# A first layer norm on rows of x, moved by selection matrices, and a first inverse stage in 64-column tiles

## The chip, the core and the metric

The kernel runs on one core of a Trainium2 chip. The metric is device time in microseconds (us). TensorE (PE) does matmuls, VectorE (DVE), ScalarE (ACT) and GpSimd (POOL) do elementwise work, SyncE (SP) issues most DMAs.

## The reference, cut to what matters

One block of a network with 2048 tokens of 512 channels: an adaptive layer norm, a long convolution per channel (an S4 layer, its kernel K made from 128 complex exponentials per channel), a second adaptive layer norm, and a feed-forward part with squared ReLU.

```python
mod = (silu(c) @ w_mod).reshape(1, 6, 1, 512)
sa, ca, ga, sb, cb, gb = mod[:, 0], ..., mod[:, 5]
h = layernorm(x) * (1 + ca) + sa               # over the 512 channels
# S4, per channel d:
P = exp(dt * A * l)                            # l = 0 .. 2047, 128 states
K = real(sum_n C * P * dt * B)
y = irfft(rfft(pad(h)) * rfft(pad(K)))[:2048] + h * Dskip
x = x + ga * y
h = layernorm(x) * (1 + cb) + sb
x = x + gb * (relu(h @ w1 + b1) ** 2 @ w2 + b2)
```

## The kernel before, in words

**Layout.** The 2048 tokens are written as 32 x 64 (a and b), and the convolution is done by two-stage transforms written as matmuls. In the layout of the transforms, a partition holds one a of one of four groups of channels, and along the free dimension stand 128 channels times 64 values of b. In the layout of rows, a partition holds one token and the free dimension its 512 channels; there are sixteen such row tiles of 128 tokens (`rows`, loaded from `xt`). The buffer `big1` holds x in the transforms' layout (`xj`, and `x_sb[c]` for one of eight blocks of 16 channels). `big0` first holds the parameters of the convolution kernel; later both hold results of the inverse transform.

**Statistics and modulation.** Mean and variance come from the row tiles (L507 to L514: bn_stats on DVE, square root on ACT). Sixteen small matmuls with slices of an identity move them to the transforms' layout (L518, L523). x itself is loaded a second time, in the transforms' layout, from `x4` (`load_x`, four loads of 1 MB). The modulation vectors come from `mod_rows` (L540), 16 matmuls with 32-column tiles each; three are needed early, three later (`late_modulation`, which also loads the last one's weights).

**Scaling.** `scale(c)` applies the layer norm to one block of 1024 elements a partition: three DVE instructions (L603 to L605) and one on POOL (L606). The gain ga / 2048 is folded in.

**Convolution kernel.** It is made in 32 units, four to a group. For each unit POOL adds the phases (L712) and multiplies three amplitude arrays (L734); ACT takes two sines (L721 to L723); DVE multiplies (L740 to L744); PE contracts over the 128 states (L751) into one half of the bank `kg`; ACT copies to `ksb` (L824), and the first transform stage follows (`stage1`, L615, evacuated at L617). Per group POOL builds integer phase tables (L684) and ACT takes 24 exponentials (L703). Buffers: three for amplitudes, two for phases, two `ksb`, three PSUM banks `ps` used in turn by everything from modulation to inverse stage, and seven `xy` buffers for rows, modulation weights and spectra, handed out by `spectrum()` and given back to the list `spectra`.

**Transforms and inverse.** `u_pieces(c)` scales a block of x and transforms it (L615, L625). `product_pieces(c)` does the second stage of the kernel's spectrum (L625), multiplies the spectra on DVE (L761) and does the first inverse stage (L769: in each bank eight matmuls with 128 columns, copied out by two ACT copies, L773). Four banks make a block, eight blocks in all. The second inverse stage (L937), the second layer norm and the feed-forward part (L1031 to L1061) follow; they make up the time from about 360 us to the end.

**The order of the work.** `background()` places the pieces of x and of the products among the 32 units, by hand-written positions. This fixes the order in which buffers are handed out. Then `keep_order` replans every engine's order: a list scheduler with a cost for each instruction (`weight`), which takes of the ready groups the one with the longest way to the end, plus a bonus (`hurry`, in ns) for some. SP's queue takes, of what is ready, the first in the order of the program. The plan is added as fixed dependencies, so each engine works through its list in order and a waiting instruction holds up all behind it.

Of the kernel before, what the change touches and what calls it, by code (L numbers as in the profile page):

```python
# [17 lines left out]
L = 2048  # L18
# [77 lines left out]
def weight(ins):  # L96
# [3 lines left out]
    if "DMA" in type(ins).__name__:  # L100
# [12 lines left out]
            tiles = 128 // cols if cols in (32, 64, 128) else 1  # L113
            t = 2.2 * max(moving / 1.2 / tiles + 2, {128: 112, 64: 28}.get(cols, 13))
            return t, t + 170
# [10 lines left out]
            if n <= 4:  # L126
                t = 200
        case "Pool":
            t = 110 + 1.8 * n
        case _:  # L130
# [4 lines left out]
def keep_order(tc, traced, slots, in_turn, whole, urgent):  # L135
# [85 lines left out]
    for g, n in enumerate(left):  # L221
        if n == 0:
            ready[of[g][0]].append(g)
    landed = table = 0
    WINDOW = 3413
# [9 lines left out]
    for _ in groups:  # L235
# [6 lines left out]
        cost = takes[g][0]  # L242
        if e == "PE":
            cost /= level(now)
            a = now
            while a < now + cost - 1:
                w = int(a // WINDOW)
                b = min(now + cost, (w + 1) * WINDOW)
                busy[w] = busy.get(w, 0) + b - a
                a = b  # L250
        elif e == "DVE" and shares_port(groups[g][0]):
            cost += min(650, max(0, free["Pool"] - now))
        elif e == "Activation":
# [23 lines left out]
def tile_adaln_ssm_ffn(  # L277
    ctx: ExitStack,
    tc: tile.TileContext,
    x4: bass.AP,  # L280
    xt: bass.AP,
# [62 lines left out]
    ctile("apart", [P, 24])  # L344

# [165 lines left out]
    mean = ctile("mean", [P, 64])  # L511
    rstd = ctile("rstd", [P, 64])
    nc.scalar.activation(mv1[:, :, 1], mv1[:, :, 1], AF.Sqrt, bias=epsb)
    nc.vector.reciprocal(mv1[:, :, 1], mv1[:, :, 1])  # L514
    mp = bank("ps", PS)
# [5 lines left out]
    moved = mp[:, 0:128].rearrange("p (g s t) -> p s g t", g=4, t=2)  # L521
    for i, t in enumerate((mean, rstd)):
        nc.vector.tensor_copy(t.rearrange("p (s g) -> p s g", g=4), moved[:, :, :, i])  # L523
    hurry(mark, 60000)

    for _ in parameters(1, NC - 1):
        pass

# [8 lines left out]
    def mod_rows(wm, ps):  # L537
        for q in range(4):
            for kc in range(4):
                nc.tensor.matmul(  # L540
                    ps[32 * q : 32 * q + 32, 0:128], srep[:, 32 * kc : 32 * kc + 32], wm[:, kc, 128 * q : 128 * q + 128],
                    start=(kc == 0), stop=(kc == 3))
# [5 lines left out]

    srep, gs = (cst.tile([P, 128], F32, tag=n, name=n) for n in ("srep", "gs"))
    nc.vector.tensor_copy(srep.rearrange("p (k x) -> p k x", k=4), bc(sl, 2, 32))  # L550
# [28 lines left out]
    nc.sync.dma_start(b1c, b1.rearrange("(t p) -> p t", p=P))  # L579
    load_x(2)  # L580
    wm_sb, wm_cb = (wm_next() for _ in range(2))
    load_x(4)
    load_x(6)

    def late_modulation():
# [12 lines left out]
        spectra.extend(wms[3:])  # L598


    def scale(c):
        ds = slice(16 * c, 16 * c + 16)
        nc.vector.tensor_sub(x_sb[c], x_sb[c], bc(mean, 1, 16))  # L603
        nc.vector.tensor_mul(x_sb[c], x_sb[c], bc(rstd, 1, 16))
        nc.vector.tensor_mul(x_sb[c], x_sb[c], bc(g4[:, ds], 2, 64))  # L605
        nc.gpsimd.tensor_add(x_sb[c], x_sb[c], bc(s4[:, ds], 2, 64))  # L606


# [146 lines left out]
    def product_pieces(c):  # L755
# [9 lines left out]
        for g in range(4):  # L765
            ps = bank("ps", PS)
            for i in range(4):
                for h, y in ((0, yu), (1, yr)):
                    nc.tensor.matmul(  # L769
                        ps[:, 128 * i : 128 * i + 128], pairs(y)[:, g, i // 2, :, i % 2],  # L770
                        e1_sb[:, h], start=(h == 0), stop=(h == 1))
            for r in range(2):
                nc.scalar.copy(  # L773
                    z4[r][c][:, :, 4 * g : 4 * g + 4].rearrange("p j d -> p d j"),
                    ps.rearrange("p (d r j) -> p d r j", d=4, r=2)[:, :, r])
# [307 lines left out]
def laid_out(inputs):  # L1083
# [41 lines left out]
```

## Time and profile before

| | |
|---|---|
| Median of 3 runs | 712.5 us (709.61 to 714.19) |
| Profiled execution | 709.58 us, its span 707.8 us, mean granted PE clock 0.928 |
| PE busy | 596.5 us (84%) |
| PE weight loads busy | 516.4 us (73%) |
| DVE busy | 392.0 us (55%) |
| ACT busy | 380.0 us (54%) |
| POOL busy | 345.3 us (49%) |
| Chain that ended last | PE 63%, POOL 20%, DMA 5%, DVE 5%, ACT 5% |

A busy share is an average over stages with different limits, so the stretches of the span are read one by one. A group of instructions is listed by line, engine, operation, output and inputs with their shapes, count, then busy us and mean ns of one, then the idle time of the engine before them and what ended it. "L12" is line 12 of the kernel. The chain of waits goes back from the last instruction, at each step to what released it. The granted PE clock is a share of the full one.

### The profile page before, as it was taken

The page shows a single profiled execution, that of the slowest core. Times are in us where ns is not written, and L with a number is a line of the kernel's source. Part 1 is how long each engine was busy: PE and PEld are TensorE (multiplying, and loading weights), DVE is VectorE, ACT ScalarE, POOL GpSimd, SP SyncE. Part 2 cuts the span into 40 slices and gives each one's busy share as a digit, 9 for nine tenths or more (in the row PEclk, how much of TensorE's full clock was granted, in tenths as well). Part 3 has the DMA queues.
Part 4 walks back from the last instruction along what each step waited for, and adds up shares of the span by engine and source line. Part 5 has one row for each costly group of instructions (what it writes and reads, how often), then busy time and mean ns, then how long its engine had stood idle before and what let it go on. Part 6 is the DMA issues. An engine that isn't in the chain of part 4 may idle for free.

```text
span 707.8 us, 18955 instructions
## 1 busy us (share of the span) xinstructions
PE 596.5 (84%) x8306; PEld 516.4 (73%) x8306; DVE 392.0 (55%) x622; ACT 380.0 (54%) x760; POOL 345.3 (49%) x316
## 2 busy tenths in 40 slices
PE   1321695766989999999868999999999999999996
PEld 1311584765989889999846788888888888888884
DVE  5788889975677576861245784243332533252233
ACT  3464867555999999875626464223432334222220
POOL 5768999999798798740969571000100000000000
PEclk9855798888999999999977999999999999999998
DMA  9990002020202022353822220001000100010001
GB/s 328 374 362 10 3 2 63 1 61 2 63 4 63 18 48 62 106 132 82 288 89 63 77 74 1 1 0 60 0 1 1 60 1 1 0 46 15 1 1 59
DMA packets 22274, 46.38 MB, mean 66 GB/s; under 512 B 3760, under 2 KB 9264, under 8 KB 20400
## 3 DMA queue, kind: packets, MB, share of 16 engines
q1 hardware_dynamic: 21760, 45.04, 20.4%
q8 instruction: 65, 1.06, 0.6%
q10 hardware_dynamic: 432, 0.14, 0.1%
q14 instruction: 17, 0.14, 0.1%
HBM read 32.58 MB, written 4.19 MB: 52 GB/s over the span
## 4 chain that ended last, share of the span: by engine, by line
PE 63%; POOL 20%; DMA 5%; DVE 5%; ACT 5%; issue 3%; DVEq 0%; SPq 0%; POOLq 0%; ACTq 0%
PE tg L1051 7%; PE tg L1053 7%; PE tg L1052 7%; PE ps L769 6%; PE ps L1031 6%; PE ps L1032 6%; PE ps L1034 5%; POOL rtl L734 5%; POOL tables L684 5%; PE ps L625 5%; POOL llph L712 4%; PE ps L615 3%; PE tg L937 2%; PE kg L751 2%; DMA xy<-xt 2%
## 5 line engine op out<-in xcount | busy, mean ns | idle before, releaser
L1039 DVE TENSOR_TENSOR xy<-xy 128x512 f32<-128x512 f32 x56 | 43.9, 784 | 158.9 <-ACT rw L1038 107.6
L1037 ACT ACTIVATE xy<-ps,b1c 128x512 f32<-128x512 f32 x42 | 29.0, 690 | 130.7 <-PE ps L1034 130.7
L966 POOL TENSOR_TENSOR big<-big,b2g 128x512 f32<-128x512 f32 x16 | 21.1, 1318 | 157.7 <-DVE xy L964 153.4
L734 POOL TENSOR_TENSOR rtl<-tables 128x512 f32<-128x512 f32 x75 | 83.9, 1142 | 8.7 <-issue 5.7
L625 PE MATMUL ps<-xy,t_sb 128*64 128x64 f32 x2048 | 71.0, 228 | 10.8 <-DVE xy L761 6.6
L769 PE MATMUL ps<-e_sb,xy 128*128 128x128 f32 x512 | 70.9, 296 | 8.4 <-ACT big L773 5.5
L625 PEld LDWEIGHTS ps<-xy,t_sb 128*64 128x64 f32 x2048 | 67.0, 143 | 14.1 <-DVE xy L761 6.9
L769 PEld LDWEIGHTS ps<-e_sb,xy 128*128 128x128 f32 x512 | 65.5, 204 | 12.0 <-ACT big L773 5.9
L712 POOL TENSOR_TENSOR llph<-tables 128x1024 int32<-128x1024 int32 x32 | 65.1, 2034 | 15.5 <-ACT tg L723 15.3
L617 ACT COPY xy<-ps 128x512 f32<-128x512 f32 x64 | 36.7, 590 | 18.9 <-PE ps L615 18.4
L743 DVE TENSOR_TENSOR rtl<-rtl,tg 128x1024 f32<-128x1024 f32 x32 | 38.9, 1217 | 14.2 <-ACT tg L723 13.4
L721 ACT ACTIVATE tg<-llph 128x1024 f32<-128x1024 int32 x32 | 33.1, 1034 | 25.0 <-POOL llph L712 20.4
L761 DVE TENSOR_TENSOR xy<-ps,xy 128x512 f32<-128x512 f32 x64 | 39.7, 681 | 7.1 <-DMA xy<-xy 6.3
L615 PE MATMUL ps<-d_sb,ksb 128*64 128x128 f32 x512 | 34.2, 281 | 7.1 <-ACT xy L617 4.2
L773 ACT COPY big<-ps 128x256 f32<-128x256 f32 x64 | 33.9, 626 | 10.4 <-PE ps L769 10.4
L615 PE MATMUL ps<-d_sb,big 128*64 128x128 f32 x512 | 33.7, 280 | 5.2 <-DVE xy L761 4.5
L723 ACT ACTIVATE tg<-llph,halfpi 128x1024 f32<-128x1024 f32 x32 | 36.0, 1126 | 1.5 <-DVE llph L744 0.9
L1031 PE MATMUL ps<-h0h,w1h 128*128 128x512 f32 x88 | 36.1, 410 | 0.0
L740 DVE SCALAR_TENSOR_TENSOR rtl<-rtl,tg 128x512 f32<-128x512 f32 x32 | 21.8, 681 | 25.4 <-ACT tg L721 12.4
L540 PE MATMUL ps<-xy,srep 128*32 128x128 f32 x192 | 19.7, 353 | 18.9 <-DMA xy<-w_mod 13.6
L615 PEld LDWEIGHTS ps<-d_sb,ksb 128*64 128x64 f32 x512 | 28.5, 140 | 9.3 <-ACT xy L617 4.7
L722 ACT ACTIVATE llph<-llph 128x1024 f32<-128x1024 int32 x32 | 34.0, 1062 | 0.3
(236 smaller groups left out, 1546.5 us busy)
## 6 DMA issues: line engine op xcount, KB each, us to landing
xy<-xt SPq DMA_DIRECT2D x32, 256.0 KB, 5.4
xy<-xy SPq DMA_DIRECT2D x16, 512.0 KB, 5.9
xy<-w_mod SPq DMA_DIRECT2D x6, 1024.0 KB, 12.4
big<-x SPq DMA_DIRECT2D x4, 1024.0 KB, 11.9
out_dram<-xy SPq DMA_DIRECT2D x16, 256.0 KB, 2.1
xy<-w SPq DMA_DIRECT2D x14, 256.0 KB, 2.8
raw<-w SPq DMA_DIRECT2D x6, 512.0 KB, 5.5
t_sb<-c_t SPq DMA_DIRECT2D x1, 2048.0 KB, 17.1
```

The source lines that it names most:

```text
L615: nc.tensor.matmul(ps[64 * r : 64 * r + 64, 128 * i : 128 * i + 128], src[:, i], d1_sb[:, r], start=True, stop=True)
L625: nc.tensor.matmul(ps[64 * r : 64 * r + 64, 64 * i : 64 * i + 64].rearrange("p (h q t) -> p q h t", h=2, t=2), t2_sb[:, 8 * g + i, r], src ...
L712: nc.gpsimd.tensor_tensor(ph.rearrange("p d r (a b) -> p (d r) a b", a=4), bc(lo[:, us].rearrange("p d r b -> p (d r) b"), 2, 4), bc(hi[:, ...
L734: nc.gpsimd.tensor_mul(o.rearrange("p d (a b) -> p d a b", a=4), bc(p, 3, 8), bc(q, 2, 4))
L761: nc.vector.tensor_mul(product_piece(y, g), ps, piece(x, g))
L769: nc.tensor.matmul(ps[:, 128 * i : 128 * i + 128], pairs(y)[:, g, i // 2, :, i % 2], e1_sb[:, h], start=(h == 0), stop=(h == 1))
L1031: pe.append(nc.tensor.matmul(ps, w1h[:, q, fs], hh[:, q, :], start=(q == 0), stop=False))
L1032: pe.append(nc.tensor.matmul(ps, wl[:, q], hh[:, q, :], start=False, stop=False))
L1039: nc.vector.tensor_mul(rr, rr, rr)
L1051: pe.append(nc.tensor.matmul(acc, r2l[:, ms], hi_, start=(t == 0), stop=False))
L1052: pe.append(nc.tensor.matmul(acc, r2h[:, ms], lo_, start=False, stop=False))
L1053: pe.append(nc.tensor.matmul(acc, r2h[:, ms], hi_, start=False, stop=(t == NF - 1)))
```

## The change

The first layer norm is done wholly on the row tiles. DVE computes (row - mean) * g1 in one instruction, where g1 = (1 + ca) * ga / 2048 now stands along the free dimension on all partitions, made by 12 matmuls with 512 columns. ACT makes a selection matrix, the identity times the token's 1 / deviation. PE first puts the shift s1 into a PSUM bank (4 matmuls of 512 columns) and then adds the row, moved to the transforms' layout, by 16 matmuls with slices of the selection matrix. ACT copies the bank to `xj`. This is done for all sixteen row tiles before any block of x is transformed. The loads of `x4`, `scale` and the moving of mean and deviation are gone. The row buffers are given back after the row steps, no longer after the statistics.

`mod_rows`, still used by the late modulation, goes through its four column tiles in the inner loop. The first inverse stage uses two 64-column tiles where it had 128 columns, and one of its two copies goes to DVE. The planner's costs, the `hurry` values and the positions of the pieces are changed.

```diff
@@ weight
-            t = 2.2 * max(moving / 1.2 / tiles + 2, {128: 112, 64: 28}.get(cols, 13))
+            t = max(1.7 * moving / tiles, 60 / tiles)
...
             if n <= 4:
-                t = 200
+                t = 150
+            elif type(ins).__name__ == "InstReciprocal":
+                t = 70 + 6.3 * n
         case "Pool":
-            t = 110 + 1.8 * n
+            t = 180 + 1.72 * n
@@ keep_order
+            kind = free_size(groups[g][0].ins[1]) if len(groups[g][0].ins) > 1 else shape
+            cost += 100 if kind != shape else 0
+            shape = kind
...
-        elif e == "DVE" and shares_port(groups[g][0]):
-            cost += min(650, max(0, free["Pool"] - now))
+        elif e == "DVE":
+            port = shares_port(groups[g][0])
+            cost += min(700, max(0, free["Pool"] - now)) if port else 0
+        elif e == "Pool":
+            cost += min(250, max(0, free["DVE"] - now)) if port else 0
@@ tile_adaln_ssm_ffn
+    picks = [ctile(f"pick{i}", [P, 128]) for i in range(2)]
...
-    def load_x(c):
-        nc.sync.dma_start(flat[1][:, 1024 * c : 1024 * c + 2048], x4[:, 1024 * c : 1024 * c + 2048])
...
-    hurry(mark, 100000)
+    hurry(mark, 30000)
...
-    spectra.extend(heads)
...
-    for g in range(4):
-        for q in range(4):
-            nc.tensor.matmul(
-                mp[32 * q : 32 * q + 32, 32 * g : 32 * g + 32], ident[:, 32 * g : 32 * g + 32],
-                mv1.rearrange("p s t -> p (s t)"), start=True, stop=True)
...
-    hurry(mark, 60000)
+    hurry(mark, 0)
...
     def mod_rows(wm, ps):
-        for q in range(4):
-            for kc in range(4):
+        for kc in range(4):
+            for q in range(4):
...
-        mod_rows(wm, m)
+        for kc in range(4):
+            nc.tensor.matmul(
+                m, sl[:, kc : kc + 1].to_broadcast([P, P]), wm[:, kc], start=(kc == 0), stop=(kc == 3))
         mps.append(m)
...
+    gs, g1, s1 = (runs(wms[2])[:, 512 * i : 512 * i + 512] for i in range(3))
+    nc.vector.tensor_scalar_mul(gs, mps[2], 1.0 / L)
+    nc.vector.scalar_tensor_tensor(g1, mps[1], 1.0, gs, op0=ALU.add, op1=ALU.mult)
+    nc.vector.tensor_mul(s1, mps[0], gs)
+
+    for s, row in enumerate(rows):
+        nc.vector.scalar_tensor_tensor(row, row, mv1[:, s, 0:1], g1, op0=ALU.subtract, op1=ALU.mult)
+        pick = picks[s % 2]
+        nc.scalar.activation(pick, ident, AF.Copy, scale=mv1[:, s, 1:2])
+        ps = bank("ps", PS)
+        for q in range(4):
+            nc.tensor.matmul(
+                ps[32 * q : 32 * q + 32, :], ident[:, 0:1].to_broadcast([P, 32]),
+                bc(s1[:, 128 * q : 128 * q + 128], 1, 4), start=True, stop=False)
+        for g in range(4):
+            for q in range(4):
+                nc.tensor.matmul(
+                    ps[32 * q : 32 * q + 32, 128 * g : 128 * g + 128], pick[:, 32 * g : 32 * g + 32],
+                    row[:, 128 * q : 128 * q + 128], start=False, stop=(g == 3))
+        nc.scalar.copy(xj[:, :, 4 * s : 4 * s + 4], ps.rearrange("p (g d) -> p d g", g=4))
+    hurry(mark, 0)
+    spectra.extend(heads)
     spectra.extend(wms)
...
-    def scale(c):
-        ds = slice(16 * c, 16 * c + 16)
-        nc.vector.tensor_sub(x_sb[c], x_sb[c], bc(mean, 1, 16))
-        nc.vector.tensor_mul(x_sb[c], x_sb[c], bc(rstd, 1, 16))
-        nc.vector.tensor_mul(x_sb[c], x_sb[c], bc(g4[:, ds], 2, 64))
-        nc.gpsimd.tensor_add(x_sb[c], x_sb[c], bc(s4[:, ds], 2, 64))
@@ product_pieces
-                    nc.tensor.matmul(
-                        ps[:, 128 * i : 128 * i + 128], pairs(y)[:, g, i // 2, :, i % 2],
-                        e1_sb[:, h], start=(h == 0), stop=(h == 1))
-            for r in range(2):
-                nc.scalar.copy(
+                    for m in range(2):
+                        nc.tensor.matmul(
+                            ps[64 * m : 64 * m + 64, 128 * i : 128 * i + 128],
+                            pairs(y)[:, g, i // 2, 64 * m : 64 * m + 64, i % 2],
+                            e1_sb[:, h], start=(h == 0), stop=(h == 1))
+            for r, copy in enumerate((nc.scalar.copy, nc.vector.tensor_copy)):
+                copy(
@@ background
-        parts = [(late, 4, 5, 1)]
-        for c in range(NC):
-            u0 = max(4 * c, 3.9) + (2 if c == 1 else 0)
-            parts.append((lambda c=c: u_pieces(c), u0, u0 + (2 if c < 2 else 2.6), 9))
-        for c in range(NC - 1):
-            u0 = 4 * c + (4 if c > 0 else 6)
-            parts.append((lambda c=c: product_pieces(c), u0, u0 + (2.5 if c == 0 else 3), 8))
+        parts = [(late, 4.75, 7.45, 1)]
+        forward = ((4.30, 4.50), (6.40, 8.00), (7.65, 10.60), (11.65, 13.85), ...)
+        back = ((6.00, 8.00), (8.00, 11.00), (12.00, 15.00), (16.00, 21.00), ...)
+        for c, (u0, u1) in enumerate(forward):
+            parts.append((lambda c=c: u_pieces(c), u0, u1, 9))
+        for c, (u0, u1) in enumerate(back):
+            parts.append((lambda c=c: product_pieces(c), u0, u1, 8))
```

More of the change, by code (lines that the diff above doesn't have):

```diff
@@ L223, in keep_order @@
             ready[of[g][0]].append(g)
-    landed = table = 0
+    landed = table = shape = 0
+    port = False
     WINDOW = 3413
@@ L279, in tile_adaln_ssm_ffn @@
     tc: tile.TileContext,
-    x4: bass.AP,
     xt: bass.AP,
@@ L342, in tile_adaln_ssm_ffn @@
     mv1 = ctile("mv1", [P, 16, 2])
+    picks = [ctile(f"pick{i}", [P, 128]) for i in range(2)]
     sts = [ctile(f"st{i}", [P, 6]) for i in range(4)]
-    ctile("apart", [P, 24])
+    rstd2 = ctile("rstd2", [P, 16])
+    ctile("apart", [P, 8])
     slots = {}
@@ L509, in tile_adaln_ssm_ffn @@
         nc.vector.bn_aggr(mv1[:, s, :], sts[s % 4])
-    spectra.extend(heads)
-    mean = ctile("mean", [P, 64])
-    rstd = ctile("rstd", [P, 64])
     nc.scalar.activation(mv1[:, :, 1], mv1[:, :, 1], AF.Sqrt, bias=epsb)
     nc.vector.reciprocal(mv1[:, :, 1], mv1[:, :, 1])
-    mp = bank("ps", PS)
-    for g in range(4):
-        for q in range(4):
-            nc.tensor.matmul(
-                mp[32 * q : 32 * q + 32, 32 * g : 32 * g + 32], ident[:, 32 * g : 32 * g + 32],
-                mv1.rearrange("p s t -> p (s t)"), start=True, stop=True)
-    moved = mp[:, 0:128].rearrange("p (g s t) -> p s g t", g=4, t=2)
-    for i, t in enumerate((mean, rstd)):
-        nc.vector.tensor_copy(t.rearrange("p (s g) -> p s g", g=4), moved[:, :, :, i])
-    hurry(mark, 60000)
-    for _ in parameters(1, NC - 1):
-        pass
+    hurry(mark, 0)
+    for c, n in ((1, 7),):
+        mark = len(nc.cur_bb.bb.instructions)
+        for _ in parameters(c, n):
+            pass
+        hurry(mark, 0)
     sl = ctile("sl", [P, 4])
@@ L547, in wm_load @@
         nc.sync.dma_start(dst, wmod_v[:, :, 512 * i : 512 * i + 512])
-    srep, gs = (cst.tile([P, 128], F32, tag=n, name=n) for n in ("srep", "gs"))
+    srep = ctile("srep", [P, 128])
     nc.vector.tensor_copy(srep.rearrange("p (k x) -> p k x", k=4), bc(sl, 2, 32))
@@ L559, in tile_adaln_ssm_ffn @@
     wm_sa, wm_ca, wm_ga = (wm_next() for _ in range(3))
-    load_x(0)
     nc.sync.dma_start(t2_sb, c_t2.rearrange("p (k r m) -> p k r m", k=32, r=2))
     nc.sync.dma_start(e1_sb, c_e1.rearrange("p (h m) -> p h m", h=2))
-    g4, s4 = (ctile(n, [P, 128]) for n in ("g4", "s4"))
     mps = []
-    for i, wm in enumerate((wm_sa, wm_ca, wm_ga)):
+    for wm in (wm_sa, wm_ca, wm_ga):
         m = bank("ps", PS)
-        mod_rows(wm, m)
+        for kc in range(4):
+            nc.tensor.matmul(
+                m, sl[:, kc : kc + 1].to_broadcast([P, P]), wm[:, kc], start=(kc == 0), stop=(kc == 3))
         mps.append(m)
-    nc.vector.tensor_scalar_mul(gs, mps[2][:, 0:128], 1.0 / L)
-    nc.vector.scalar_tensor_tensor(g4, mps[1][:, 0:128], 1.0, gs, op0=ALU.add, op1=ALU.mult)
-    nc.vector.tensor_mul(s4, mps[0][:, 0:128], gs)
+    gs, g1, s1 = (runs(wms[2])[:, 512 * i : 512 * i + 512] for i in range(3))
+    mark = len(nc.cur_bb.bb.instructions)
+    nc.vector.tensor_scalar_mul(gs, mps[2], 1.0 / L)
[16 more added lines that the diff above has]
+        nc.scalar.copy(xj[:, :, 4 * s : 4 * s + 4], ps.rearrange("p (g d) -> p d g", g=4))
+    hurry(mark, 0)
+    spectra.extend(heads)
     spectra.extend(wms)
@@ L579, in tile_adaln_ssm_ffn @@
     nc.sync.dma_start(b1c, b1.rearrange("(t p) -> p t", p=P))
-    load_x(2)
     wm_sb, wm_cb = (wm_next() for _ in range(2))
-    load_x(4)
-    load_x(6)
     def late_modulation():
@@ L642, in u_pieces @@
     def u_pieces(c):
-        scale(c)
-        yield
         xs = xus[c] = spectrum()
@@ L794, in background @@
     def background():
-        parts = [(late, 4, 5, 1)]
-        for c in range(NC):
-            u0 = max(4 * c, 3.9) + (2 if c == 1 else 0)
-            parts.append((lambda c=c: u_pieces(c), u0, u0 + (2 if c < 2 else 2.6), 9))
-        for c in range(NC - 1):
-            u0 = 4 * c + (4 if c > 0 else 6)
-            parts.append((lambda c=c: product_pieces(c), u0, u0 + (2.5 if c == 0 else 3), 8))
+        parts = [(late, 4.75, 7.45, 1)]
+        forward = ((4.30, 4.50), (6.40, 8.00), (7.65, 10.60), (11.65, 13.85), (16.65, 18.60), (20.40, 21.60), (24.40, 26.35), (28.15, 30.60))
+        back = ((6.00, 8.00), (8.00, 11.00), (12.00, 15.00), (16.00, 21.00), (20.00, 23.00), (24.00, 28.25), (29.00, 31.50))
+        for c, (u0, u1) in enumerate(forward):
+            parts.append((lambda c=c: u_pieces(c), u0, u1, 9))
+        for c, (u0, u1) in enumerate(back):
+            parts.append((lambda c=c: product_pieces(c), u0, u1, 8))
         todo = sorted(
@@ L912, in tile_adaln_ssm_ffn @@
     nf, ng = (spectra[i].tensor.name for i in (5, 6))
-    mv = ctile("mean", [P, 16, 2])
-    rstd2 = ctile("rstd", [P, 16])
+    mv = mv1
     x2 = zj[0].rearrange("p c (s q) d -> p s q c d", q=4)
@@ L1087, in laid_out @@
     arrays = {
-        "x4": x.transpose(2, 0, 3, 1).reshape(128, 8192),
         "xt": x.reshape(32, 16, 4, 512).transpose(1, 2, 0, 3).reshape(16, 128, 512),
```

## The prediction

> **What bounds the kernel now.** I read the busy slices of the page first, then cut the span into stretches where the busiest engine changes, and asked for the busy time of each stretch. The columns are PE, PE's weight loads, DVE, ACT and POOL with instruction counts, then the granted PE clock.
>
> ```profile
> core 0: us, PE busy (x) PEld busy (x) DVE busy (x) ACT busy (x) POOL busy (x), PEclk, DMA share, GB/s
> 0.00:63.00 63.00, 12.84 (x136) 10.69 (x136) 49.81 (x114) 29.96 (x84) 42.26 (x57) 0.78 0.83 301
> 63.00:180.00 117.00, 80.64 (x1802) 73.84 (x1804) 92.60 (x111) 76.10 (x163) 115.08 (x99) 0.80 0.09 20
> 180.00:332.00 152.00, 147.14 (x3628) 138.26 (x3624) 99.42 (x157) 136.06 (x263) 108.29 (x106) 1.00 0.26 64
> 332.00:400.00 68.00, 54.92 (x1400) 44.91 (x1396) 28.57 (x65) 36.95 (x73) 47.52 (x34) 0.82 0.44 138
> 400.00:707.80 307.80, 300.93 (x1350) 248.74 (x1349) 121.58 (x177) 100.96 (x179) 32.18 (x23) 0.99 0.06 19
> ```
>
> From 63 to 180 us POOL has 115.1 of 117 us: it makes the convolution kernel's phases and amplitudes, and everyone else waits for it. From 180 to 332 us PE has 147.1 of 152, with ACT close behind at 136.1. After 400 us PE is full with the feed-forward part, which the change does not touch. So the gain, if any, comes out of the POOL stretch, and a little out of the PE stretch.
>
> How far POOL holds back the rest shows in the exponentials, which ACT runs once for every group of four units. The timeline of ACT has these starts:
>
> ```profile
> 75.30 3.69 ACT L703 ACTIVATE tables<-big 128x64 f32<-128x64 f32 x24
> ...
> 167.30 3.69 ACT L703 ACTIVATE tables<-big 128x64 f32<-128x64 f32 x24 [3.90 <-POOL rtl L734]
> ...
> 227.89 3.69 ACT L703 ACTIVATE tables<-big 128x64 f32<-128x64 f32 x24
> ```
>
> There are two groups between each of these rows: 92.0 us in the POOL stretch, 60.6 us later. At the later pace the first pair would be 31 us shorter.
>
> **Why POOL is slow there.** The same POOL instructions, first from 60 to 180 us and then from 180 to 340 us (count, busy, mean ns):
>
> ```profile
> L734 POOL TENSOR_TENSOR rtl<-tables 128x512 f32<-128x512 f32 x26 | 32.6, 1273 | 0.2 <-PE kg L751 0.2
> L712 POOL TENSOR_TENSOR llph<-tables 128x1024 int32<-128x1024 int32 x12 | 25.6, 2135 | 0.2
> L606 POOL TENSOR_TENSOR big<-big,s 128x1024 f32<-128x1024 f32 x8 | 17.1, 2144 | 0.0
> L684 POOL TENSOR_TENSOR tables<-tables 128x128 int32<-128x128 int32 x16 | 10.5, 655 | 0.6
> ...
> L684 POOL TENSOR_TENSOR tables<-big 128x128 int32<-128x128 int32 x8 | 5.3, 674 | 0.0
> L684 POOL TENSOR_TENSOR tables<-big,tables 128x128 int32<-128x128 int32 x4 | 5.0, 1261 | 0.1
> ...
> L706 POOL TENSOR_TENSOR tables<-tables,big 128x256 f32<-128x256 f32 x4 | 4.0, 992 | 0.2
> ```
>
> ```profile
> L734 POOL TENSOR_TENSOR rtl<-tables 128x512 f32<-128x512 f32 x42 | 44.0, 1073 | 8.5 <-issue 5.7 <-PE kg L751 2.7
> L712 POOL TENSOR_TENSOR llph<-tables 128x1024 int32<-128x1024 int32 x18 | 35.2, 1956 | 15.3 <-ACT tg L723 15.3
> ...
> L684 POOL TENSOR_TENSOR tables<-tables 128x128 int32<-128x128 int32 x12 | 5.1, 426 | 0.5
> ...
> L684 POOL TENSOR_TENSOR tables<-big 128x128 int32<-128x128 int32 x6 | 2.6, 433 | 0.0
> ...
> L706 POOL TENSOR_TENSOR tables<-tables,big 128x256 f32<-128x256 f32 x3 | 1.9, 649 | 0.2
> ...
> L684 POOL TENSOR_TENSOR tables<-big,tables 128x128 int32<-128x128 int32 x3 | 1.6, 541 | 0.0
> ```
>
> Every form is slower in the first list. The surplus is 26 x 0.200 + 12 x 0.179 + 16 x 0.229 + 8 x 0.241 + 4 x 0.720 + 4 x 0.343 = 17.2 us. What DVE does only in the first stretch are the three steps of `scale`, all with two SBUF sources:
>
> ```profile
> L603 DVE TENSOR_TENSOR big<-big,mean 128x1024 f32<-128x1024 f32 x8 | 17.0, 2127 | 0.0
> ...
> L605 DVE TENSOR_TENSOR big<-big,g 128x1024 f32<-128x1024 f32 x8 | 14.8, 1846 | 0.0
> ...
> L604 DVE TENSOR_TENSOR big<-big,rstd 128x1024 f32<-128x1024 f32 x8 | 13.9, 1738 | 0.2
> ...
> L1060 DVE TENSOR_TENSOR xy<-xy,big 128x512 f32<-128x512 f32 x16 | 10.3, 687 | 0.0
> ```
>
> **Part 1, `scale` goes.** POOL loses L606: 8 x 2.144 = 17.1 us, all inside the stretch where nothing covers it. DVE loses 45.7 us in 24 instructions. With them goes the surplus on POOL, at most 17.2 us, at least nothing if it has another cause; I take all of it, because later, without them, it is not there. The x4 loads go too; the stretch that they load (DMA share 0.83 up to 63 us) is ahead of POOL's bound, so I count nothing for them.
>
> **Part 2, sixteen row steps come.** DVE does one scalar_tensor_tensor of 128x512 per row, again with two SBUF sources; nearest is L1060, 0.69 us, 11 us in all. The 24 old instructions cost POOL 17.2 / 24 = 0.72 us each. Sixteen at that price are 11.5 us, but they lie at about 36 to 75 us, and up to 63 us POOL works only 42.3 us of 63. I take +8 (bounds 0 and 11.5). "SBUF — State Buffer" of the Trainium skill, section "SBUF: two separate sides", says that POOL and a DVE instruction with two SBUF inputs exclude each other for a whole instruction; by that, sixteen waits of at most 0.69 us give 11 us, and the contention is lessened by this change, not removed. The slower forms above agree with it.
>
> ACT builds a 128x128 selection per row and copies the bank out:
>
> ```profile
> L617 ACT COPY xy<-ps 128x512 f32<-128x512 f32 x64 | 36.7, 590 | 18.9 <-PE ps L615 18.4 <-DVE xy L761 0.3
> ...
> L773 ACT COPY big<-ps 128x256 f32<-128x256 f32 x64 | 33.9, 626 | 10.4 <-PE ps L769 10.4
> ...
> L977 ACT ACTIVATE xy<-ps,sbc,cbc 128x128 f32<-128x128 f32 x42 | 16.1, 461 | 12.6 <-PE ps L970 12.6
> ```
>
> That is 0.59 + 0.46 = 1.05 us a row, 17 us, in a time when ACT has room (30.0 of 63 us).
>
> PE does 4 matmuls of 512 columns for the shift and 16 of 128 for the selection, each in 32-column tiles, four tiles in turn. Rows of the timeline for its price and place:
>
> ```profile
> 22.00 5.64 PE L540 MATMUL ps<-xy,srep 128*32 128x128 f32 x64 [13.58 <-DMA xy<-w_mod]
> ...
> 34.34 0.25 DVE L514 RECIPROCAL mv<-mv 128x16 f32<-128x16 f32 x1 [2.34 <-ACT mv L513]
> ...
> 37.04 4.50 PE L540 MATMUL ps<-xy,srep 128*32 128x128 f32 x32 [1.74 <-DVE rstd L523]
> ...
> 70.28 1.95 PE L751 MATMUL kg<-rtl,llph 128*32 128x64 f32 x64 [5.27 <-DVE ksb L825]
> ...
> 72.16 1.98 PE L615 MATMUL ps<-d_sb,ksb 128*64 128x128 f32 x16
> ...
> 96.56 1.09 PE L615 MATMUL ps<-d_sb,big 128*64 128x128 f32 x16
> ...
> 102.28 1.12 PE L751 MATMUL kg<-rtl,llph 128*32 128x64 f32 x64
> ```
>
> A matmul in f32 stands as two records (the third modulation has 16 matmuls and stands at 37.04 as x32). L540 keeps to one column tile for four matmuls: 88 ns a record. L751 changes tile from record to record, at half the moving columns: 17.5 ns, or 30 at the slow clock. So 32 records of the selection are between 32 x 17.5 = 0.56 and 32 x 88 = 2.8 us, and the 8 records of the shift, with four times the columns, between 0.7 (four tiles at once) and 2.8. One row is 1.3 to 5.6 us; I take 1.7 at the full clock and 2.6 with the slow one mixed in, as the order of the loops is that of L751. Sixteen are 42 us. They begin when the statistics are done (34.6 us here) and the three modulations, now 24 records of 512 columns: 24 x 4 x 88 ns = 8.4 us if they scale as L540, which took 8.4 for its 96. The third no longer waits for the bank that the statistics held (37.04). So the rows run from about 36 to 78 us.
>
> Behind them waits the first stage of the convolution kernel, L615: its banks come after those of the sixteen rows in the same ring of three, and its spectrum buffer is one that held rows. It began at 72.2 us, so it is 6 us late. POOL does not see this at once, since three amplitude buffers, two `kg` halves and two `ksb` lie between; I take +5 (bounds -9, if a row costs 1.7, and +54, at 5.6). The transforms of x began at 96.6 us and are not held up. On SP's queue the loads for the second modulation now wait for the rows' buffers; only late modulation needs them, and its place moves from 4 to 4.75 or later. The exchanges behind them (L654) follow x's second stage, later still.
>
> Front: -17.1 - 17.2 + 8 + 5 = -21 us. Does the rest fit? In the 117 us PE had 80.6 and ACT 76.1; with 15 us of row steps and without part of the modulations PE has about 90 in 96 at the same mean clock. It is tight, but a fuller PE had clock 1.00 in the next stretch.
>
> **Part 3, first inverse stage in 64 columns.** From the chain of waits (start, us, line):
>
> ```profile
> 202.57 1.97 PE ps L615 x32
> ...
> 209.69 0.88 PE ps L615 x16
> ...
> 214.66 2.08 PE ps L769 x16
> ...
> 303.06 3.98 PE ps L769 x32
> ```
>
> A bank becomes 32 records shaped as L615: 1.76 (2 x 0.88) to 1.97 us, against 2.08. Two banks of L769 in a row take 3.98, not 4.16, so 0.18 us of a lone one goes with entering and leaving. Saved are 0.11 to 0.41 us a bank; I take 0.2. "TensorEngine Tiling" of the Trainium skill, section "Key Properties", says that changing the tiling mode drains TensorE; by that the whole 0.18 goes where L769 stood between 64-column work, and the sum would be 3 us better. The 0.18 agrees with it. Of the 32 banks 27 lie after 180 us: 27 x 0.2 = -5 us (-3 to -11). One of two copies moves to DVE: ACT loses 27 x 0.53 = 14 us in that stretch (33.9 / 64 each), DVE gains 9 to 19 (half to all of L1060's 0.69 each) on its 99.4 of 152, so both stay under PE.
>
> **Part 4, the planner.** New costs and `hurry` values reorder every engine. No row prices that; I take 0, bounds +-6 (half of the 13 us that PE idles from 332 to 400). The late modulations, 96 more records as L540, now take their tiles in turn: PE may save three quarters of 8.4 us there, under POOL's cover, which I count as 0.
>
> **The sum.** The profiled execution took 709.6 us (span 707.8, 1.8 around it), 2.9 below the median 712.5. 709.6 - 21 - 5 = 683.6; for a median of runs I add the 2.9 and get 687, rounded up.
>
> **Rivals.**
> Forecast, 0.56: 675 to 699. The unknowns are some 4 us for the contention, 8 for the gate, 4 for the inverse stage and 6 for the order; taken as independent they make 12.
> PE and ACT take over at once, 0.18: POOL's 34 us go, but the row steps and PE's waits for banks hold the groups. For it: PE and ACT are full just after 180 us. Against: 60.6 us for two groups is already their pace. The front gives 6, the inverse stage 5: 702.
> All of it, 0.13: no contention from the rows and no late start: -34 - 11 = -45, so 667.
> Order only, 0.07: the new plan gives back what POOL saves: 712, within 6.
> Slower, 0.06: the row stage itself is the gate. At 5.6 us a row it ends at 126 us, 54 after 72.2; less 39 saved that is +15, 728. It decides from 72.2 + 39 = 111 us, that is 4.7 us a row. Against: it needs column tiles that do not overlap, and L751 shows that they do.
>
> About 1%, 7 us, is what a measurement of this kernel can tell from no change. Under 705.4: all of the forecast, two thirds of the second, the third: 0.82. Within: 0.10. Above: 0.08. The range 664 to 707 leaves out order only, slower, and the tails.
>
> **What would show it.** Right: no POOL row of the scaled x, L734 back near 1073 ns before 180 us except beside row steps, groups of four about 30 us apart from the third on, row steps over by about 78 us, inverse-stage banks at 1.8 to 1.97 us, PE full from about 155 us. Wrong: L615 of the convolution kernel starting after 100 us; POOL waiting for PE or DVE ahead of 100 us; PE idle between 80 and 150 us with ACT or DVE as releaser; the stretch after 332 us longer than 376 us.

## The result and the profile after

The changed kernel takes 680.75 us (median of 4 runs, 679.91 to 683.87) against 711.75 us for the kernel before (709.61 to 714.19). The ratio is 0.9569, with a 95% interval of 0.9531 to 0.9608: 31 us less. The forecast was 687. The profiled execution took 683.87 us with a span of 682.0; the sum of the prediction for it was 683.6. That is nearer than its terms deserve: the experiments below give several of them other sizes.

The stretches of the span, cut as before; the columns are again PE, its weight loads, DVE, ACT and POOL, then the granted clock:

```profile
core 0: us, PE busy (x) PEld busy (x) DVE busy (x) ACT busy (x) POOL busy (x), PEclk, DMA share, GB/s
0.00:63.00 63.00, 29.12 (x280) 15.52 (x284) 50.08 (x109) 31.94 (x94) 34.71 (x51) 0.90 0.65 218
63.00:180.00 117.00, 106.58 (x2998) 93.42 (x2992) 90.19 (x143) 108.42 (x235) 109.39 (x112) 0.98 0.16 39
180.00:332.00 152.00, 136.66 (x3656) 129.15 (x3656) 95.36 (x160) 116.40 (x209) 101.92 (x99) 0.99 0.33 90
```

From 63 to 180 us no engine is alone at its limit any more: POOL has 109.4 of 117 us, ACT 108.4 (76.1 before), PE 106.6 (80.6 before). Before 63 us POOL does less than it did (34.7 against 42.3); two waits behind this are shown below.

The exponentials of the groups three to seven on ACT's timeline:

```profile
85.52 3.69 ACT L707 ACTIVATE tables<-big 128x64 f32<-128x64 f32 x24
114.99 3.70 ACT L707 ACTIVATE tables<-big 128x64 f32<-128x64 f32 x24
144.30 3.69 ACT L707 ACTIVATE tables<-big 128x64 f32<-128x64 f32 x24
175.71 3.69 ACT L707 ACTIVATE tables<-big 128x64 f32<-128x64 f32 x24
202.11 3.68 ACT L707 ACTIVATE tables<-big 128x64 f32<-128x64 f32 x24
```

Group three starts 10.2 us later than before, but the two groups that took 92.0 us take 58.8, so group five is 23.0 us early. The second inverse stage begins at 332.6 instead of 357.5 us (24.9 early), and the span ends 25.8 early. So the gain of the profiled pair stands in the POOL stretch, and the stretches behind it keep it. (This pair is the fastest run of before beside the slowest of after; the medians differ by 31.)

POOL's forms from 60 to 180 us:

```profile
L738 POOL TENSOR_TENSOR rtl<-tables 128x512 f32<-128x512 f32 x35 | 37.0, 1075 | 1.8 <-PE kg L755 1.8
L716 POOL TENSOR_TENSOR llph<-tables 128x1024 int32<-128x1024 int32 x16 | 31.8, 1986 | 2.4 <-ACT tg L727 2.1
```

The amplitudes are back at 1075 ns (1273 before, 1073 in the later stretch of before), the phases at 1986 (2135). The row steps on PE's timeline, from the first to the last:

```profile
22.44 12.37 PE L564 MATMUL ps<-xy,sl 128*128 128x512 f32 x24 [9.52 <-DMA xy<-w_mod]
...
45.26 1.93 PE L579 MATMUL ps<-xy,ident 128*32 128x512 f32 x8 [10.45 <-DVE xy L571]
46.97 1.93 PE L584 MATMUL ps<-xy,pick 128*32 128x128 f32 x32
...
51.07 1.03 PE L579 MATMUL ps<-xy,ident 128*32 128x512 f32 x8
51.93 1.05 PE L584 MATMUL ps<-xy,pick 128*32 128x128 f32 x32
52.80 1.03 PE L579 MATMUL ps<-xy,ident 128*32 128x512 f32 x8
...
60.34 1.94 PE L584 MATMUL ps<-xy,pick 128*32 128x128 f32 x32 [3.04 <-ACT pick L576]
...
83.22 1.09 PE L621 MATMUL ps<-d_sb,ksb 128*64 128x128 f32 x16
...
85.13 1.06 PE L584 MATMUL ps<-xy,pick 128*32 128x128 f32 x32
```

A row costs 52.80 - 51.07 = 1.73 us at the full clock. But the rows start at 45.3, not 36, and the last ends at 86.2, not 78. PE had waited 10.45 us for the gain and shift vectors (L569 to L571), and in between it waits for DVE and ACT. DVE, which is busy all this while, shows why:

```profile
38.73 0.24 DVE L518 RECIPROCAL mv<-mv 128x16 f32<-128x16 f32 x1
...
41.42 0.67 DVE L744 SCALAR_TENSOR_TENSOR rtl<-rtl,tg 128x512 f32<-128x512 f32 x1
...
44.53 0.68 DVE L571 TENSOR_TENSOR xy<-ps,xy 128x512 f32<-128x512 f32 x1
45.12 6.55 DVE L574 SCALAR_TENSOR_TENSOR xy<-xy,mv,xy 128x512 f32<-128x512 f32 x5
51.59 0.61 DVE L464 SCALAR_TENSOR_TENSOR big<-big 128x448 f32<-128x448 f32 x1
52.13 0.74 DVE L574 SCALAR_TENSOR_TENSOR xy<-xy,mv,xy 128x512 f32<-128x512 f32 x1
52.79 0.61 DVE L472 SCALAR_TENSOR_TENSOR big<-big 128x448 f32<-128x448 f32 x1
53.44 2.95 DVE L475 RECIPROCAL big<-big 128x448 f32<-128x448 f32 x1
```

The modulations were done at 34.8 us and the statistics at 39.0 (L518), but the vectors stand in DVE's list behind the first convolution unit (L744), and the rows alternate with the parameters of the later blocks (L464 to L475), for which POOL waits 12.85 us:

```profile
63.31 0.94 POOL L494 TENSOR_TENSOR big<-big 128x448 int32<-128x448 int32 x1 [12.85 <-DVE big L465]
```

Last, the front also begins late: in the changed kernel two small loads stand the other way round on ACT's queue, `log_dt` now second, and the first DVE step of the kernel's tables waits 6.86 us for it (2.72 before; it started at 3.68):

```profile
7.81 0.17 DVE L420 TENSOR_SCALAR kf<-ldt 128x4 f32<-128x4 f32 x1 [6.86 <-DMA ldt<-log_dt]
```

The order of the loads is not the work of the new costs alone: a_old_plan below, with the old costs, has `log_dt` second too, and b_new_plan, with the new ones, has it first. And 7.81 is the latest of five traces that have it second (5.60 to 7.81).

### The profile page after: what moved, and what is told of

The parts are those of the page before. It is cut to its first block, busy times and chain, and to the rows that moved or that the text cites. A ratio compares the mean times of both kernels' runs of the same rounds, so it can differ in the third digit from the quotient of the medians.

```text
span 682.0 us, 21080 instructions
## 1 busy us (share of the span) xinstructions
PE 606.8 (89%) x9354; PEld 512.2 (75%) x9354; DVE 382.4 (56%) x644; ACT 378.6 (56%) x760; POOL 313.8 (46%) x308
## 4 chain that ended last, share of the span: by engine, by line
PE 66%; ACT 14%; DVE 13%; issue 4%; POOL 2%; DMA 1%; DVEq 0%; SPq 0%; ACTq 0%
PE tg L1056 7%; PE tg L1058 7%; PE tg L1057 7%; PE ps L1036 6%; PE ps L1037 6%; PE ps L1039 6%; PE ps L631 6%; PE ps L621 5%; PE ps L774 4%; ACT tables L707 3%; PE kg L755 2%; DVE xy L574 2%; PE kg L1036 2%; PE kg L1037 2%; PE kg L1039 2%
## 5 line engine op out<-in xcount | busy, mean ns | idle before, releaser
L1044 DVE TENSOR_TENSOR xy<-xy 128x512 f32<-128x512 f32 x56 | 41.8, 747 | 158.0 <-ACT rw L1043 107.1
L738 POOL TENSOR_TENSOR rtl<-tables 128x512 f32<-128x512 f32 x75 | 79.2, 1079 | 18.0 <-PE kg L755 17.6
L631 PE MATMUL ps<-xy,t_sb 128*64 128x64 f32 x2048 | 68.7, 224 | 5.5 <-issue 2.6
L774 PE MATMUL ps<-e_sb,xy 128*64 128x128 f32 x1024 | 62.3, 275 | 6.0 <-issue 2.4
L716 POOL TENSOR_TENSOR llph<-tables 128x1024 int32<-128x1024 int32 x32 | 63.4, 1983 | 8.7 <-ACT tg L727 7.7
L774 PEld LDWEIGHTS ps<-e_sb,xy 128*64 128x64 f32 x1024 | 57.0, 140 | 8.1 <-issue 2.6
L779 DVE COPY big<-ps 128x256 f32<-128x256 f32 x32 | 19.3, 603 | 54.5 <-ACT big L779 54.3
L621 PE MATMUL ps<-d_sb,ksb 128*64 128x128 f32 x512 | 35.7, 282 | 5.3 <-DVE ksb L831 2.2
L621 PEld LDWEIGHTS ps<-d_sb,big 128*64 128x64 f32 x512 | 29.0, 141 | 7.0 <-ACT xy L623 2.6
L1042 ACT ACTIVATE xy<-kg,b1c 128x512 f32<-128x512 f32 x14 | 9.6, 689 | 39.9 <-PE kg L1039 39.9
```

Source lines behind the costliest of these rows:

```text
L621: nc.tensor.matmul(ps[64 * r : 64 * r + 64, 128 * i : 128 * i + 128], src[:, i], d1_sb[:, r], start=True, stop=True)
L631: nc.tensor.matmul(ps[64 * r : 64 * r + 64, 64 * i : 64 * i + 64].rearrange("p (h q t) -> p q h t", h=2, t=2), t2_sb[:, 8 * g + i, r], src ...
L716: nc.gpsimd.tensor_tensor(ph.rearrange("p d r (a b) -> p (d r) a b", a=4), bc(lo[:, us].rearrange("p d r b -> p (d r) b"), 2, 4), bc(hi[:, ...
L738: nc.gpsimd.tensor_mul(o.rearrange("p d (a b) -> p d a b", a=4), bc(p, 3, 8), bc(q, 2, 4))
L774: nc.tensor.matmul(ps[64 * m : 64 * m + 64, 128 * i : 128 * i + 128], pairs(y)[:, g, i // 2, 64 * m : 64 * m + 64, i % 2], e1_sb[:, h], st ...
L1044: nc.vector.tensor_mul(rr, rr, rr)
```

## The experiments

Four readings of each trace, in us, place what follows: the starts of the exponentials of groups three and five, that of the second inverse stage, and the span.

| kernel | group 3 | group 5 | second inverse | span |
|---|---|---|---|---|
| before | 75.3 | 167.3 | 357.5 | 707.8 |
| b_no_pool_add | 75.1 | 158.4 | 352.3 | 701.1 |
| b_no_dve_scale | 72.5 | 144.7 | 334.2 | 685.1 |
| b_no_scale | 72.5 | 140.4 | 330.0 | 680.0 |
| b_new_plan | 75.4 | 151.2 | 343.4 | 691.4 |
| b_new_no_scale | 72.1 | 138.1 | 328.8 | 678.8 |
| a_old_plan | 86.4 | 150.3 | 341.3 | 691.0 |
| after | 85.5 | 144.3 | 332.6 | 682.0 |
| e1_128_held | 83.5 | 142.4 | 331.3 | 681.1 |
| act_copies | 84.7 | 143.1 | 337.1 | 685.9 |
| ldt_held | 82.8 | 141.6 | 326.3 | 678.2 |
| no_shift_held | 83.8 | 142.6 | 327.6 | 677.0 |
| rows_first | 88.8 | 149.0 | 336.9 | 687.2 |
| params_first | 93.6 | 161.5 | 351.2 | 703.6 |

Where a name ends in "held", in the three that begin with "b_no" and in b_new_no_scale, the order on every engine is that of the kernel that was edited (but for the swap in ldt_held), so that only the edited work differs. In the others the planner orders anew.

### What `scale` cost: b_no_pool_add, b_no_dve_scale, b_no_scale

In the kernel before, `scale` is cut down to 8 elements an instruction: POOL's alone, DVE's three alone, all four. Most of the shift, of the normalisation, or of both is then left out.

```diff
-        nc.gpsimd.tensor_add(x_sb[c], x_sb[c], bc(s4[:, ds], 2, 64))
+        nc.gpsimd.tensor_add(x_sb[c][:, 0:1, 0:8], x_sb[c][:, 0:1, 0:8], bc(s4[:, 16 * c : 16 * c + 1], 2, 8))
```

> The kernel before, with the POOL add of the layer norm's shift (L606) cut from 1024 elements to 8, so that most of the shift is left out; every engine's order is that of before. Theory A (POOL sets the pace from 63 to 180 us): the 17.1 us of L606 go from the total, 693 to 698 us in place of 712. Rival B (PE, ACT and DVE take over at once): at most 5 us go, 707 or more.

> The kernel before, with the three DVE instructions of scale (L603 to L605) cut from 1024 elements to 8, so that most of the normalisation is left out; POOL's add stays, orders are those of before. Theory A: the forms of POOL go back to their later lengths (L734 1273 to about 1073 ns) and the surplus of 17 us goes from the total, 694 to 699 us. Rival C (the surplus has another cause, and DVE is hidden): L734 stays above 1200 ns, 708 to 712 us.

> The kernel before, with all four instructions of scale cut to 8 elements; orders as before. Theory A: 34 us go together, 677 to 683 us. Rival B: 8 us or less, 704 or more. What lies between the two shows where the next bound begins.

Measured: without POOL's step 700.46 us (ratio 0.9872, 0.9839 to 0.9905), 8.9 less than the kernel before beside it; without DVE's 687.07 (0.9680, 0.9657 to 0.9702), 22.3 less; without all 679.96 (0.9576, 0.9551 to 0.9601), 29.4 less. POOL's forms from 60 to 180 us, without POOL's step:

```profile
L737 POOL TENSOR_TENSOR rtl<-tables 128x512 f32<-128x512 f32 x26 | 31.7, 1236 | 5.9 <-PE kg L754 5.9
L715 POOL TENSOR_TENSOR llph<-tables 128x1024 int32<-128x1024 int32 x14 | 28.5, 2037 | 4.2 <-ACT tg L726 4.0
```

and without DVE's steps:

```profile
L737 POOL TENSOR_TENSOR rtl<-tables 128x512 f32<-128x512 f32 x33 | 35.1, 1084 | 0.2
...
L608 POOL TENSOR_TENSOR big<-big,s 128x1024 f32<-128x1024 f32 x8 | 15.2, 1908 | 0.0
L687 POOL TENSOR_TENSOR tables<-tables 128x128 int32<-128x128 int32 x16 | 6.7, 420 | 0.6
```

The contention is shown: with the three DVE steps gone, the forms fall to their later level (1084 ns, and 420 where 655 stood), though POOL does all its own work. With POOL's step gone and DVE's kept they stay slow (1236). This agrees with "SBUF — State Buffer" of the Trainium skill, section "SBUF: two separate sides": a DVE instruction with two SBUF inputs holds off POOL for a whole instruction, and the other way round.

The two parts are not worth what the prediction gave them. POOL's 17.1 us are worth 8.9: 5.9 us of waiting for PE's `kg` and 4.2 for ACT come in their place, which were not there before (0.2 and 0.2 in the same forms). DVE's three steps, priced at their 17.2 us of surplus on POOL, are worth 22.3. Part of the rest is a form that the sum left out, POOL's own step of `scale`, which falls from 2144 to 1908 ns (8 x 0.236 = 1.9 us); what makes up the other 3 us is not shown.

### What the plan was worth: b_new_plan, a_old_plan

The first is the kernel before with nothing but the new `weight` and `keep_order`. The second is the changed kernel with the old ones. `hurry` values and positions stay those of each kernel.

```diff
 # b_new_plan, as the change has it
-            t = 2.2 * max(moving / 1.2 / tiles + 2, {128: 112, 64: 28}.get(cols, 13))
+            t = max(1.7 * moving / tiles, 60 / tiles)
...
-            t = 110 + 1.8 * n
+            t = 180 + 1.72 * n
```

> The kernel before with the planner's new costs (weight and the rules of keep_order) and nothing else of the change. Theory A: within 6 us of before, 706 to 718. Rival D (the gain is the planner's): 700 or less.

> The changed kernel with the planner's costs and rules of before (hurry values and positions stay as changed). The new plan alone took 15 us off the kernel before. Theory I (plan and layer norm are separate gains and add up): 694 to 698 us. Theory J (both close the same gap in the POOL stretch): 681 to 688.

Measured: the new costs alone 694.17 us (0.9780, 0.9756 to 0.9803), 15.2 less than before; the change without them 697.84 (0.9833, 0.9789 to 0.9877), 11.4 less by the medians. The two sum to about 27, and together they gave 31. Put in first, the new costs are worth 15.2; put in last, on top of all the rest, 17.1 (697.84 to 680.75). Half of the gain, then, comes from cost figures in a planner, which change no instruction of the kernel. It isn't contention that the new order avoids; POOL's forms of b_new_plan from 60 to 180 us:

```profile
L743 POOL TENSOR_TENSOR rtl<-tables 128x512 f32<-128x512 f32 x30 | 39.7, 1334 | 0.1
L721 POOL TENSOR_TENSOR llph<-tables 128x1024 int32<-128x1024 int32 x14 | 31.4, 2240 | 0.2
L615 POOL TENSOR_TENSOR big<-big,s 128x1024 f32<-128x1024 f32 x4 | 9.6, 2395 | 0.0
```

Each is as slow as before or slower (1334 against 1273), but only four of the eight scaled blocks fall into the stretch, where all eight did. POOL makes 30 amplitude arrays of this form there instead of 26. Which of the new costs does this was not tried.

### The norm for nothing under the new plan: b_new_no_scale

b_new_plan with `scale` cut down as in b_no_scale, its order kept.

```diff
 # on b_new_plan, the four steps of scale as in b_no_scale
-        nc.vector.tensor_sub(x_sb[c], x_sb[c], bc(mean, 1, 16))
+        nc.vector.tensor_sub(x_sb[c][:, 0:1, 0:8], x_sb[c][:, 0:1, 0:8], bc(mean[:, 0:8], 1, 1))
...
```

> The kernel before with the new plan (694.2 us), its orders held, and all four instructions of scale cut to 8 elements, so that most of the normalisation is left out. Theory I: the 29 us that this took from the old plan go again, 663 to 667 us. Theory J: 15 us or less go, 679 or more. What the changed kernel (680.8) lies above this is the price of its row steps, less what the inverse stage brings.

Measured: 679.64 us (0.9575, 0.9554 to 0.9596). Under the old costs a norm for nothing gave 29.4 us, under the new ones 14.5. And with the norm left out, the new costs are worth nothing: 679.96 us under the old ones, 679.64 under the new. So what the new costs gain hangs on the steps of `scale` being there. The reading that fits is that moving these blocks out of POOL's stretch and deleting them take the same time out, so it cannot be had twice; that both kernels run into one next limit near 680 us is not ruled out. In the table, group five goes from 151.2 (new plan) to 138.1 with the norm gone, and to 144.3 in the changed kernel: up to there the row steps give back 6.2 of 13.1 us.

### The inverse stage: e1_128_held, act_copies

The first goes back to 128-column matmuls in the first inverse stage and keeps the split copies and the order. The second keeps the tiles and puts both copies on ACT.

```diff
 # e1_128_held
-                    for m in range(2):
-                        nc.tensor.matmul(ps[64 * m : 64 * m + 64, ...], ...)
+                    nc.tensor.matmul(ps[:, 128 * i : 128 * i + 128], ...)
 # act_copies
-            for r, copy in enumerate((nc.scalar.copy, nc.vector.tensor_copy)):
+            for r, copy in enumerate((nc.scalar.copy, nc.scalar.copy)):
```

> The changed kernel with the first inverse stage in 128 columns again, its copies still one on ACT and one on DVE, orders as in the changed kernel. By the prediction a bank costs PE 0.2 us more, 27 banks in the stretch that PE bounds: 5 us, 684 to 687 us. If the 64-column tiles are worth nothing: 680 to 682.

> The changed kernel with both copies of a first inverse bank on ACT again, 64-column tiles kept; the planner reorders some 10 to 30% of the rows of DVE and ACT. In the changed kernel the DVE copy starts only after the ACT copy of the same bank, so a bank comes free no earlier; what the split brings is ACT's 17 us. If ACT holds nothing up there: 680 to 682 us. If it does: 684 or more.

Measured: 128 columns 683.2 us (0.9606, 0.9588 to 0.9624), so the tiles are worth some 2.5 us, with intervals that overlap (0.9531 to 0.9608 for the changed kernel). Both copies on ACT: 687.01 (0.9688, 0.9670 to 0.9705), so the split is worth 6.3 by medians, 8.5 by ratios. The groups of the changed kernel show that the split copies don't even run side by side:

```profile
L774 PE MATMUL ps<-e_sb,xy 128*64 128x128 f32 x1024 | 62.3, 275 | 6.0 <-issue 2.4
...
L779 DVE COPY big<-ps 128x256 f32<-128x256 f32 x32 | 19.3, 603 | 54.5 <-ACT big L779 54.3
```

DVE starts its half only when ACT's copy is through: 54.3 us of waiting, all on DVE. The two copies write different buffers (`z4[0]` and `z4[1]`) and share only the bank that they read. "PSUM — Partial Sum Buffer" of the Trainium skill, section "PSUM bank collisions raise a hardware error", says that a compiler's scheduler adds a dependency between instructions on different engines that touch the same bank in the same 32 partitions, reads too; the trace agrees. So a bank is not free sooner; what changes is ACT's load. The stretch from 180 to 332 us in act_copies:

```profile
180.00:332.00 152.00, 135.20 (x3596) 127.99 (x3598) 86.70 (x140) 123.14 (x226) 96.18 (x89) 0.96 0.31 83
```

ACT has 123.1 us there against 116.4, and in the table act_copies stands level with the changed kernel at group five (143.1 and 144.3) and 4.5 us behind at the second inverse stage. That ACT's list is what costs them is argued from this, not shown: the order was planned anew in act_copies, and the granted clock was 0.96 against 0.99 in that stretch.

### What sets the row stage's end: ldt_held, no_shift_held, params_first, rows_first

Four edits of the changed kernel: the `log_dt` load ahead of `cvec` again; the shift's matmuls cut from 512 to 32 columns, which leaves the shift out; POOL's later parameters hurried; the row steps hurried. The last two have `log_dt` first as well.

```diff
 # no_shift_held
-                ps[32 * q : 32 * q + 32, :], ident[:, 0:1].to_broadcast([P, 32]), bc(s1[...], 1, 4), ...)
+                ps[32 * q : 32 * q + 32, 0:32], ident[:, 0:1].to_broadcast([P, 32]), bc(s1[...], 1, 4), ...)
 # params_first: after the parameters; rows_first: after the row steps
-    hurry(mark, 0)
+    hurry(mark, 100000)
```

> The changed kernel with the first two loads on ACT's queue in the order of before (log_dt ahead of c); all else in the same order. In the changed kernel log_dt lands 4.1 us later than before and the first exponentials start 4.5 us later. Theory E (the late start goes through to the end): 676 to 677.5 us in place of 680.8. Rival F (the row steps and the loads of w_mod, which don't move, absorb it): 680 to 681.

> The changed kernel with the four shift matmuls of each row step cut from 512 to 32 columns, so that the shift s1 is left out of h; orders as in the changed kernel. PE is spared about 0.8 us a row, 12 us in all. Theory G (the row steps on PE are the gate for the first transform stage): that stage starts 8 to 12 us earlier than 83.2 us and 5 us or more go from the total, 676 or less. Rival H (DVE's order, row steps ahead of the parameters, sets the start): the stage starts within 4 us of 83.2, the total is 679 to 681.

> The changed kernel with log_dt loaded first and the parameters of the seven later groups put ahead of the row steps by the planner (a bonus of 100000 ns). By rival H of the run without the shift, POOL gets its parameters about 5 us earlier than at 63.3 us and the third group of exponentials starts 7 to 10 us before 85.5: 671 to 675 us. By theory G the row steps come later and with them the first transform stage: 680 or more.

> The changed kernel with log_dt loaded first and the row steps put ahead by the planner (bonus 100000 ns): DVE does its sixteen in one block, before the later groups' parameters. With the parameters ahead the total was 706. Theory G (the end of the row steps gates the first transform stage, and that gates POOL): the stage starts about 10 us before 80.5 and the total is 670 to 676. Rival K (POOL's later parameters, some 10 us later, decide): 683 or more. If both weigh alike: 677 to 682.

Measured: ldt_held 679.28 us (0.9563, 0.9524 to 0.9602), not to be told from the changed kernel. Its group three is 2.7 us earlier than in the changed kernel's trace, but only 0.7 us earlier than in that of e1_128_held (83.5), which has the changed kernel's order and loads and in which `log_dt` came earlier (its first use was at 5.85 us). no_shift_held 680.03 (0.9575, 0.9552 to 0.9598), no gain, and its group three (83.8) is not before that of e1_128_held: PE's time for the rows isn't what holds them. params_first 706.24 (0.9932, 0.9907 to 0.9957), 25 us worse. rows_first 691.41 (0.9745, 0.9724 to 0.9766), 11 worse. POOL in params_first, the whole span:

```profile
L742 POOL TENSOR_TENSOR rtl<-tables 128x512 f32<-128x512 f32 x75 | 80.1, 1092 | 32.4 <-PE kg L759 32.2
```

The rows come later, the first stage of the convolution kernel starts at 94.2 us instead of 83.2, and POOL waits 32.2 us for PE (17.6 in the changed kernel). The other way round, in rows_first, POOL waits for the parameters, 3.2 us longer than in ldt_held, which has the same loads (there the step starts at 60.59 us):

```profile
63.76 0.93 POOL L498 TENSOR_TENSOR big<-big 128x448 int32<-128x448 int32 x1 [15.96 <-DVE big L469]
```

This points at DVE's list in the first 65 us, which feeds PE's rows and POOL's parameters by turns, as the gate: pushing either side forward starves the other, and the changed kernel's mixture is the best of the three. It is argued, not shown, since the planner ordered every engine anew in these two. None of the kernels tried is clearly faster than the changed one.

## Why the prediction was right, and where not

**What bounds the kernel** held. POOL's stretch was the place of the gain, 23.0 of the profiled pair's 25.8 us, and the surplus on POOL was DVE's doing.

**Part 1, -34.** Taken together it was nearly right: a norm for nothing under the old plan gave 29.4. The split was wrong. POOL's step counted one for one, because "nothing covers it"; it was worth 8.9 of 17.1, since a POOL with 115 of 117 us busy hid waits for PE and ACT that came up as soon as it got ahead (5.9 and 4.2 us). DVE's steps were worth more than what they cost POOL.

**Part 2.** The price of a row at the full clock, 1.7 us, was measured as 1.73, and the stage took 41 us, as forecast (42). Its place was wrong, 45 to 86 us instead of 36 to 78. The failing step is "they begin when the statistics are done and the three modulations": it asked when the inputs exist and not where DVE's list puts the vectors and the rows. The late gate was 10.2 us at group three, not +5; 0.7 to 2.7 us of it go with the order of the two loads (ldt_held beside e1_128_held and the changed kernel). The modulations took 12.4 us, not 8.4. The contention from the rows, +8, did not come to POOL's stretch as far as the forms show. It fell on DVE instead, whose row step took 1.07 us in the mean, not 0.69: the five of the row above from 45.12 us took 1.31 each, those from 52.13 to 62.15, while POOL waited for the parameters, 0.70 to 0.75. POOL's own steps beside the first five stretched too (L460 took 1.47 us, where the like L458 just before took 1.13), but it was about to wait 12.85 us in any case.

```profile
L574 DVE SCALAR_TENSOR_TENSOR xy<-xy,mv,xy 128x512 f32<-128x512 f32 x16 | 16.6, 1070 | 0.0
```

With everything but the costs, a_old_plan has group five 17.0 us early, against the front's -21, in a run of 692.82 us, where its median is 697.84. On top of the new costs the same part brings 6.9 (151.2 to 144.3). Over the whole kernel, front and inverse stage together, forecast as -26, were worth 11.4 us under the old costs and 13.4 under the new (694.17 to 680.75).

**Part 3, -5.** The chain of the changed kernel has the banks at 1.75 to 1.97 us, as forecast (start, us, line):

```profile
244.26 1.97 PE ps L774 x32
247.10 1.75 PE ps L774 x32
```

The tiles were worth about half of the 5. "TensorEngine Tiling" of the Trainium skill, section "Key Properties", says that a change of tiling mode drains TensorE; the prediction made 3 us more of that, and 2.5 us for all of it does not show such a gain. The copy moved to DVE, counted 0 since ACT stayed under PE, was worth 6 to 8.

**Part 4, 0 within 6.** This is the step that failed most: the planner's costs alone were worth 15.2 us, more than twice the bound. The bound was taken from PE's idle time after 332 us, but the plan worked in POOL's stretch.

So 683.6 came out by luck, because misses offset each other: parts 1 to 3 were put at -26 and gave 11.4 to 13.4 us, and part 4 was put at 0 and gave 15.2 to 17.1. Under the old costs a norm for nothing gives 29.4 us and the change with these costs (a_old_plan) 11.4, inverse stage included: there the row steps give back 18 us or more, where +13 was forecast. Under the new costs a norm for nothing gives only 14.5 us, and the change 13.4. The sum for the median, 687, lay 6 us over 680.75.

**The rivals.** PE and ACT taking over was half true: both are nearly full from 63 us, yet two groups now need 58.8 us. "Order only" had the sign of the planner's part wrong. "Slower" named a real mechanism and a wrong point. It was to decide from a kernel stage at 111 us; params_first, at 94.2, had already lost all but 5 of the 31 us, in a run where POOL waited 32.2 us for PE in spite of its three amplitude buffers. **The signs**: groups 29 to 31 us apart and 1075 ns were right; the rows' end was not. One sign of "wrong" did come up, POOL waiting for DVE ahead of 100 us (12.85 us, 7.02 before), and it showed the true weak point. From the second inverse stage on the kernel takes 349.4 us (350.3 before), as forecast.

**Still open**: the norm's move alone, in one run, without the inverse stage and under the new costs. By subtraction it is worth some 4 us (ratio 0.9780 to 0.9569, less 0.0037 for the tiles and 0.0119 for the copies), but the parts do not add up well enough here to trust that, and the price of the copies comes from a kernel that was planned anew.

## What to carry to other kernels

Where a change comes with new planner costs, price them by themselves: put the new costs on the old kernel. Here that was half the gain, and it hung on the very steps that the change removed: without them the new costs were worth nothing. Ask of a moved step not only when its inputs exist but what stands ahead of it in its engine's list, and who else that engine feeds. And an engine that is busy 115 of 117 us need not give back one for one what is taken from it; a run with the one operation cut down, the order kept, gives the price.

## What the runs showed that was not expected

- The modulation as 512-column matmuls at one column tile of 128 took 12.37 us for 24 records. The first five start 0.85 to 1.02 us apart, the others 0.43 to 0.48, at a granted clock of 1.00 from 22.4 to 34.8 us; why the first are slow is not shown. A row's shift, 8 records of 512 columns over four 32-column tiles, took 0.86 us (51.07 to 51.93), 0.11 us a record, a quarter of 0.43. So the four tiles in turn overlapped in full.
- ACT and DVE copied 128x256 from PSUM in the same time, 602 and 603 ns.
- Two small loads on one queue, issued some 0.4 us apart: over all fourteen traces the first use of `log_dt` was at 3.4 to 3.7 us where it was loaded first, and at 5.6 to 7.8 where it was second.
- The chain of the changed kernel holds stalls of about 2 us on PE that no releaser explains, with 9354 matmul records instead of 8306:

```profile
267.22 1.96 issue
...
299.38 2.39 issue
...
312.33 2.19 issue
```

From 180 to 332 us such stalls make 6.6 us in the changed kernel, 2.8 in e1_128_held, whose first inverse stage has half the matmuls, and 0.4 in the kernel before. What they are was not tried.
